# A gated attention and a low-rank mixer on one core: scores computed for the upper triangle only, transposes by DMA, and an order made by a list scheduler

## The chip, the cores and the metric

The kernel runs on one core of a Trainium2 chip. The metric is the device time of one execution in microseconds (us). Engines: TensorE (PE, with its weight loads as PEld), VectorE (DVE), ScalarE (ACT), GpSimd (POOL) and SyncE (SP, which here only issues DMAs). The one slow execution seen here (of e5) took 2.3% longer than that kernel's median. The batches ran on different chips; the kernel before took 1374.2 to 1375.3 us (medians) in all of them.

## The reference

Eight sequences of S = 3136 rows, width D = 256; z has 64 columns.

```python
scores = (1.0 / S) * z @ z.T              # symmetric, 3136 x 3136 for each sequence
attn   = maximum(scores, 0) ** 2          # symmetric too
x      = u * (attn @ v)
h      = (x.T @ U @ V).T                  # U: S x 32, V: 32 x S
uu     = x + h
out    = uu + maximum(uu @ w1, 0) @ w2    # w1: 256 x 1024, w2: 1024 x 256
```

Rows are handled in 25 tiles of 128 (the last has 64 rows). `attn` is symmetric: block (i, j) is the transpose of block (j, i). The change builds on this.

## The kernel before

All 25 x 25 blocks of the scores are computed, in groups of 512 columns, each as a matmul of 128 rows of contraction of which the upper 64 are zero. The mixer of a sequence follows its attention, and x is transposed by matmuls with an identity.

```python
for gi, (g0, gw) in enumerate(igroups):                       # groups of 512 columns
    for jp in range(0, NT, 2):
        for jj in range(npair):
            nc.tensor.matmul(out=ps_s[:, jj, :gw],
                             lhsT=zzT[:, (jp + jj) * P : (jp + jj + 1) * P],
                             rhs=zzT[:, g0 : g0 + gw], start=True, stop=True)
        # relu: every fourth on DVE, the others on ACT; then the square on DVE
        nc.scalar.activation(out=attn_sb[...], in_=ps_s[...], func=AF.Relu)
        nc.vector.tensor_tensor(out=attn_sb[...], in0=attn_sb[...], in1=attn_sb[...], op=ALU.mult)
    for qq in range(nq):                                      # attention times v
        for jt in range(NT):
            nc.tensor.matmul(out=ps_o[:, qq, :], lhsT=attn_sb[:, jt, q * P : (q + 1) * P],
                             rhs=v_bf[:, jt, :], start=(jt == 0), stop=(jt == NT - 1))
    # ... x_bf = ps_o * u; after all groups: t1 = U^T x
# mixer: x transposed by matmul and V^T t1 added in PSUM; then w1, relu on ACT, w2, add, store
nc.tensor.matmul(out=ps_u2[:, db, ...], lhsT=x_bf[:, it, db * P : (db + 1) * P], rhs=ident, ...)
# ...
emit_prep(0)
for b in range(B):
    emit_attention(b)
    if b + 1 < B:
        emit_prep(b + 1)
    emit_mixer(b)
```

## Time and profile before

| | before |
|---|---|
| time, median of 3 | 1374.39 us |
| TensorE busy | 96% of the span, at the full granted clock |
| ACT, DVE busy | 58%, 52% |
| DMA queue | 20.7% of 16 engines |
| one sequence | 168 us |

The page of the kernel before: engines with busy time, the busy tenths of 40 slices of the span, the DMA queue, and the chain of work that ended last by engine and line.

```profile
PE 1317.1 (96%) x9865; PEld 913.3 (67%) x10008; DVE 707.9 (52%) x1104; ACT 792.9 (58%) x976; POOL 23.7 (2%) x41
PE   3999999999999999999999999999999999999998
PEclk9999999999999999999999999999999999999999
DMA  9611421124111241111411115111121111111101
...
q1 hardware_dynamic: 109440, 86.41, 20.7%
...
PE 75%; ACT 21%; DMA 2%; issue 1%; DVE 1%; ACTq 0%; SPq 0%; POOL 0%
ACT relu_sb L277 12%; ACT attn_sb L184 4%; ACT u2T_bf L260 3%; ACT zzT L135 2%; DMA v_raw<-in_v_dram 1%; PE ps_6060 L202 0%; PE ps_4297 L202 0%; PE ps_11349 L202 0%; PE ps_7477 L202 0%; PE ps_2188 L202 0%; PE ps_12766 L202 0%; PE ps_11003 L
```

TensorE is busy for 90% or more of every slice but the first and the last, and the clock digit is 9 (full) throughout. The chain of the next view, in order of time (start, duration, what), gives the durations of matmuls in a steady stream:

```profile
207.46 3.07 PE ps_2015 L202 x28
...
330.31 0.86 PE ps_3405 L270 x4
```

28 matmuls of 256 columns take 3.07 us, 0.109 us from start to start; four of 512 columns 0.86 us, 0.216 us from start to start. The copy of t1, made once per sequence, shows the rhythm (count, durations in ns, first and last start):

```profile
L231 ACT CAST t_sb<-ps_3083 x1: 373/373/373, 305.6 to 305.6; 128x256 bf16<-128x256 f32 x1
L231 ACT CAST t_sb<-ps_4846 x1: 372/372/372, 473.5 to 473.5; 128x256 bf16<-128x256 f32 x1
```

473.5 - 305.6 = 167.9 us per sequence. At the two durations above, a sequence's 371,200 matmul columns need about 158 us, so bubbles are few and only less TensorE work can help much.

### The profile page before, as it was taken

The numbers are of one execution on the slowest core, as the hardware profiler recorded it, in microseconds if no ns is written. First come the engines' busy times: TensorE is split into PE (matmuls) and PEld (weight loads), VectorE is DVE, ScalarE is ACT, GpSimd is POOL, SyncE is SP. The second block draws the span as 40 slices with busy tenths as digits, with TensorE's granted clock in tenths as the row PEclk, the third lists the DMA queues.
The fourth block names the chain that finished last, engine by engine and source line by source line (L and its number), as shares of the span: only waits on it lengthen the run. The fifth ranks groups of instructions, "written<-read, shape, count | busy, mean of one in ns | idle before, by whom it ended". The sixth has DMA issues, their size and how long they took to land.

```text
span 1373.0 us, 22895 instructions
## 1 busy us (share of the span) xinstructions
PE 1317.1 (96%) x9865; PEld 913.3 (67%) x10008; DVE 707.9 (52%) x1104; ACT 792.9 (58%) x976; POOL 23.7 (2%) x41
## 2 busy tenths in 40 slices
PE   3999999999999999999999999999999999999998
PEld 1677666676666766667666676666766667666665
DVE  1776147751477414774157732677217772177721
ACT  6854855557555575556655565655655555455554
POOL 2000000000000000000000000000000000000000
PEclk9999999999999999999999999999999999999999
DMA  9611421124111241111411115111121111111101
GB/s 238 181 32 30 146 71 32 32 64 134 49 32 32 65 146 43 31 32 57 148 49 32 32 49 157 41 32 32 57 102 33 32 32 34 62 34 32 32 32 65
DMA packets 109542, 87.89 MB, mean 64 GB/s; under 512 B 32832, under 2 KB 109120, under 8 KB 109440
## 3 DMA queue, kind: packets, MB, share of 16 engines
q1 hardware_dynamic: 109440, 86.41, 20.7%
q8 instruction: 78, 1.28, 0.4%
q14 instruction: 24, 0.20, 0.0%
HBM read 60.70 MB, written 25.69 MB: 63 GB/s over the span
## 4 chain that ended last, share of the span: by engine, by line
PE 75%; ACT 21%; DMA 2%; issue 1%; DVE 1%; ACTq 0%; SPq 0%; POOL 0%
ACT relu_sb L277 12%; ACT attn_sb L184 4%; ACT u2T_bf L260 3%; ACT zzT L135 2%; DMA v_raw<-in_v_dram 1%; PE ps_6060 L202 0%; PE ps_4297 L202 0%; PE ps_11349 L202 0%; PE ps_7477 L202 0%; PE ps_2188 L202 0%; PE ps_12766 L202 0%; PE ps_11003 L202 0%; PE ps_9240 L202 0%; PE ps_5714 L202 0%; PE ps_2534 L202 0%
## 5 line engine op out<-in xcount | busy, mean ns | idle before, releaser
L202 PEld LDWEIGHTS <-attn_sb 128*128 128x128 bf16 x5000 | 466.9, 98 | 164.3 <-DVE attn_sb L189 61.9
L189 DVE TENSOR_TENSOR attn_sb<-attn_sb 128x1024 bf16<-128x1024 bf16 (+3 forms) x728 | 407.0, 608 | 73.7 <-ACT attn_sb L184 71.4
L169 PEld LDWEIGHTS <-zzT 128*128 128x128 bf16 x1400 | 133.3, 98 | 107.2 <-issue 29.3
L297 PEld LDWEIGHTS <-relu_sb 128*128 128x128 bf16 x1600 | 148.6, 98 | 50.5 <-ACT relu_sb L277 24.0
L270 PEld LDWEIGHTS <-w_bf 128*128 128x128 bf16 x896 | 83.2, 98 | 87.2 <-issue 7.8
L150 ACT CAST v_bf<-v_raw 128x1024 bf16<-128x1024 f32 (+1 forms) x56 | 52.0, 965 | 24.0 <-DMA v_raw<-in_v_dram 15.5
L246 PEld LDWEIGHTS <-x_bf 128*128 128x128 bf16 x400 | 30.3, 97 | 10.7 <-issue 4.5
L128 PEld LDWEIGHTS <-z_bf 128*128 128x128 bf16 x200 | 16.1, 102 | 26.3 <-issue 22.5
L289 PEld LDWEIGHTS <-V_bf 128*128 128x128 bf16 x200 | 19.3, 98 | 6.4
L223 PEld LDWEIGHTS <-U_bf 128*128 128x128 bf16 x200 | 19.6, 98 | 2.2
L212 POOL MEMSET u_sb<- 128x256 f32 x8 | 2.5, 311 | 1047.3 <-DVE x_bf L214 1047.3
L128 PE MATMUL ps_124<-ident,z_bf 128*128 128x128 bf16 x4 | 0.6, 299 | 19.7 <-ACT z_bf L121 19.7
L120 POOL MEMSET z_bf<- 128x1600 bf16 x8 | 11.4, 1431 | 80.8 <-PE ps_6732 L253 13.6
L121 ACT ACTIVATE z_bf<-z_raw 128x1600 bf16<-128x1600 f32 x8 | 12.4, 1550 | 0.0
L253 PEld LDWEIGHTS <-t_sb 128*128 128x128 bf16 x112 | 10.9, 97 | 1.4 <-issue 1.1
L305 DVE TENSOR_TENSOR out_sb<-ps_1522,x_bf 128x512 f32<-128x512 f32 x1 | 0.7, 692 | 16.8 <-PE ps_1522 L297 16.8
L305 DVE TENSOR_TENSOR out_sb<-ps_6811,x_bf 128x512 f32<-128x512 f32 x1 | 0.7, 692 | 16.7 <-PE ps_6811 L297 16.7
L305 DVE TENSOR_TENSOR out_sb<-ps_8574,x_bf 128x512 f32<-128x512 f32 x1 | 0.7, 692 | 16.7 <-PE ps_8574 L297 16.7
L305 DVE TENSOR_TENSOR out_sb<-ps_5048,x_bf 128x512 f32<-128x512 f32 x1 | 0.7, 690 | 16.7 <-PE ps_5048 L297 16.7
L305 DVE TENSOR_TENSOR out_sb<-ps_10337,x_bf 128x512 f32<-128x512 f32 x1 | 0.7, 692 | 16.7 <-PE ps_10337 L297 16.7
L305 DVE TENSOR_TENSOR out_sb<-ps_3285,x_bf 128x512 f32<-128x512 f32 x1 | 0.7, 690 | 16.7 <-PE ps_3285 L297 16.7
L305 DVE TENSOR_TENSOR out_sb<-ps_12100,x_bf 128x512 f32<-128x512 f32 x1 | 0.7, 690 | 16.7 <-PE ps_12100 L297 16.7
(2728 smaller groups left out, 2817.8 us busy)
## 6 DMA issues: line engine op xcount, KB each, us to landing
v_raw<-in_v_dram SPq DMA_DIRECT2D x48, 512.0 KB, 4.8
u_sb<-in_u_dram SPq DMA_DIRECT2D x96, 256.0 KB, 2.6
out_dram<-out_sb SPq DMA_DIRECT2D x96, 256.0 KB, 2.1
z_raw<-in_z_dram SPq DMA_DIRECT2D x8, 768.0 KB, 5.3
wtmp<-in_moe_w_ch_dram SPq DMA_DIRECT2D x4, 512.0 KB, 3.8
v_raw<-in_v_dram SPq DMA_DIRECT2D x8, 64.0 KB, 2.2
u_sb<-in_u_dram SPq DMA_DIRECT2D x8, 64.0 KB, 2.1
out_dram<-out_sb SPq DMA_DIRECT2D x8, 64.0 KB, 2.0
```

The costliest lines, as they stand in the source:

```text
L135: nc.scalar.copy(out=zzT[:, tg * P : (tg + n_in_g) * P], in_=pz[:, : n_in_g * P],)
L150: nc.scalar.copy(out=v_bf[:, c0 : c0 + cn, :], in_=v_raw[:, :cn, :])
L169: nc.tensor.matmul(out=ps_s[:, jj, :gw], lhsT=zzT[:, (jp + jj) * P : (jp + jj + 1) * P], rhs=zzT[:, g0 : g0 + gw], start=True, stop=True,)
L184: nc.scalar.activation(out=attn_sb[:, jp : jp + npair, :gw], in_=ps_s[:, :npair, :gw], func=AF.Relu,)
L189: nc.vector.tensor_tensor(out=attn_sb[:, jp : jp + npair, :gw], in0=attn_sb[:, jp : jp + npair, :gw], in1=attn_sb[:, jp : jp + npair, :gw] ...
L202: nc.tensor.matmul(out=ps_o[:, qq, :], lhsT=attn_sb[:, jt, q * P : (q + 1) * P], rhs=v_bf[:, jt, :], start=(jt == 0), stop=(jt == NT - 1),)
L223: nc.tensor.matmul(out=pt1[:, 0, :], lhsT=U_bf[:, it, :], rhs=x_bf[:, it, :], start=(it == 0), stop=(it == NT - 1),)
L246: nc.tensor.matmul(out=ps_u2[:, db, q * P : (q + 1) * P], lhsT=x_bf[:, it, db * P : (db + 1) * P], rhs=ident, start=(q == 0), stop=False,)
L260: nc.scalar.copy(out=u2T_bf[:, :, c0 : c0 + cw], in_=ps_u2[:, :, :cw])
L270: nc.tensor.matmul(out=ps_m1[:, hh, :cw], lhsT=w1_bf[:, db, ht * P : (ht + 1) * P], rhs=u2T_bf[:, db, c0 : c0 + cw], start=(db == 0), stop ...
L277: nc.scalar.activation(out=relu1_sb[:, hp : hp + 2, :cw], in_=ps_m1[:, :, :cw], func=AF.Relu,)
L297: nc.tensor.matmul(out=ps_f[:, qq, :], lhsT=relu1_sb[:, ht, q * P : (q + 1) * P], rhs=w2_bf[:, ht, :], start=False, stop=(ht == NH - 1),)
```

## The change

The kernel is rewritten. Its intent:

1. Scores only for the upper triangle and for the tail row of blocks. z lies twice in SBUF, in partitions 0 to 63 and 64 to 127, so that two matmuls of 64 rows of contraction run side by side in the two halves of the array.
2. The lower triangle comes from DMA transposes, SBUF to SBUF, of the squared blocks; so do z^T and the mixer's input. TensorE does no transposes.
3. Each step is a task. A list scheduler, run when the program is built, simulates the engines with fitted durations and fixes every engine's order; the mixer of one sequence fills TensorE's gaps in the next attention.
4. Squared scores live in 64 slots of 512 columns. All loads but a few of the first sequence, and all stores, are issued on POOL.

The diff has over 1100 lines; these are its core (cuts marked).

```diff
+NSLOT = 64
+def t_mm(n):
+    return n / 2400.0 + 0.0025
 ...
+            s = sq[c, k] = add(f"sq{b}.{c}.{k}", {"DVE": t_dve(cols)}, ..., deps=[it.relu], ...)
 ...
+                    ts = tslot[c, k]
+                    tr[c, k] = add(
+                        f"tr{b}.{c}.{k}", {"SP": 0.25 + 0.12 * blocks},
+                        lambda K, t, ...: K.tr_quad(t, q, ts, k, cols),
+                        deps=[s], prio=0.5, pipe=0.18 * blocks, use=[q, ts],
+                    )
 ...
+    def score(self, t, row, col0, cols, zT):
+        z = self.zT[zT.i]
+        a = slice(64 * t.half, 64 * t.half + 64)
+        self.nc.tensor.matmul(
+            out=self.pair[t.pref.i][:, t.half, :cols],
+            lhsT=z[a, row * P : (row + 1) * P], rhs=z[a, col0 : col0 + cols], start=True, stop=True,
+        )
 ...
+    def tr_quad(self, t, q, ts, k, cols):
+        a = P if k == 0 else 0
+        self.nc.sync.dma_start_transpose(
+            out=self.q[ts.i][:, a:cols].rearrange("p (t r) -> p t r", r=P), in_=self.q[q.i][:, a:cols]
+        )
 ...
+    plan = make_plan()
+    with tc.manual_schedule():
+        bufs = Bufs(tc.nc, ctx, tc, u, v, z, moe_U, moe_V, moe_w_ch1, moe_w_ch2, out)
+        for t in plan.order:
+            t.emit(bufs, t)
```

## The prediction

> **What bounds it now.** TensorE. The page gives matmul busy 96% of 1373.0 us at granted clock 1.00; ACT 58%, DVE 52%, DMA queue 1 20.7%. The timeline shows a steady rhythm: the t1 copy recurs every 168 us, one sequence. Counting columns of the matmuls: 371,200 per sequence (scores 80,000, attention times v 160,000, mixer products 102,400, the rest transposes by matmul, t1 and V products). The chain of waits has 28 matmuls of 256 columns in 3.07 us (0.109 us each) and four of 512 in 0.86 us (0.216 us). At these rates the work is about 158 us, so only some 10 us per sequence are bubbles, plus about 27 us of start. Less TensorE work is the only large lever.
>
> **What the change does to TensorE, per sequence (estimates from those two durations).**
> - Scores: only the upper triangle and the tail row, 41,600 columns in place of 80,000, and with 64-deep contraction on row halves two run at once. The Trainium skill, "TensorEngine Tiling (Array Packing)", section Tiling Modes / Key Properties, allows two 64-row tiles in parallel and says that changing the mode drains the array; no run here shows it yet. About 46 pairs: 10 us, plus 3 to 4 us for some 17 mode changes (0.2 us each, my guess). Before: 34 us.
> - z and x transposes go to DMA: 4 us off. The added V product in the transposed layout and its repetition in the output group fall into one 25-matmul product: about 3 us off. t1 on four column groups: 1.5 us in place of 2.7.
> - Attention times v stays: 625 x 0.109 = 68 us. Mixer products stay: 43.4 us.
> Sum: about 129 us in place of 158. Eight times: 1033 us.
>
> **What moves elsewhere.** DMA gains, per sequence, 363 transposed 128x128 bf16 blocks (25 z, 276 scores, 24 half ones for the tail, 50 u), 11.9 MB. At the 261 GB/s of the skill's "DMA: Bandwidth & Descriptors", section Latency and other measured facts, that is 46 us (an estimate; no run shows it); the plain 10.8 MB at the page's rate (86.41 MB in 20.7% of the span, 304 GB/s) is 36 us. Together 82 us of about 130: not a bound unless transposes cost twice that. ACT and DVE: score relus fall from 643 us to about 390, squares from 407 to about 225, the PSUM copies (28 + 48 us) vanish, x+h adds and casts bring about 90 us; some 1130 us on two engines, about 52% each. Not a bound.
>
> **Critical path.** All TensorE savings lie on it. The mixer of one sequence is laid into the next attention, so relu waits there (ACT relu_sb is 12% of the chain) should be covered. Start shrinks to about 12 us (weights load later). The last mixer runs alone: about 12 us of fill and drain. Static order, transposes landing late and single-slot buffers will cost stalls: 4% of 1033, about 40 us.
>
> **Predicted: 1095 us, range 1055 to 1165. Faster by over 2%: 0.96; within: 0.02; slower: 0.02.**
>
> **Right if:** TensorE stays over 90% busy with about 129 us of work per sequence; 1400 score matmuls become 728, overlapped in pairs; attention times v still 5000 at 0.109 us; DMA busy near 65%, transposes landing in 2 to 4 us. **Wrong if:** idle before attention times v is put down to transposes (DMA over 85% or landing over 6 us, SP issue the limit); score pairs do not overlap; DVE over 75% busy; loads from POOL late[...]; the last mixer costs over 70 us.

## The result, and the profile after

The changed kernel took 1263.22 us (median of 4 runs, 1258.97 to 1267.25; before, 1374.4 us). The ratio of the fast runs is 0.9194, 95% interval 0.917 to 0.9217: 8% faster, where 20% was predicted. A ratio is the mean time of one kernel's fast runs over that of the other's in the same rounds, so it is not quite the ratio of the medians. Executions over 1.5% slower than the fastest of the same kernel are left out of the means.

The page of the changed kernel, the same lines, the two big DMA queues (q1: issued by SP, q0: by POOL), and the group of transposes among the DMA issues (count, median us from issue to landing):

```profile
PE 1084.5 (86%) x8533; PEld 770.1 (61%) x8624; DVE 611.3 (48%) x1400; ACT 513.0 (41%) x817; POOL 177.9 (14%) x247
PE   1646793899988999889987999868989899899998
PEclk9968897999988999999988999989999999999999
DMA  8487864976669957797569867798568885577232
...
q1 hardware_dynamic: 401648, 97.70, 46.7%
q0 software_dynamic: 24496, 83.97, 25.1%
...
PE 57%; DMA 21%; issue 14%; DVE 2%; SPq 2%; POOL 2%; ACT 2%; POOLq 0%; ACTq 0%; DVEq 0%
...
q<-q SPq DMA_TRANSPOSE x664, 3.2
```

TensorE is no longer always busy (86%; the prediction asked for over 90%), its clock digits drop to 6 to 8 in places, DMA takes 21% of the chain where it took 2%, and the DMA engines are 46.7 + 25.1 = 72% busy. A table by stretch of time (start:end, length, busy time of each engine, granted clock, DMA share, GB/s) shows where:

```profile
0.00:45.00 45.00, 8.41 (x31) 2.26 (x32) 14.28 (x42) 16.47 (x28) 4.62 (x10) 1.00 0.72 151
90.00:135.00 45.00, 32.01 (x204) 19.91 (x204) 15.03 (x38) 12.05 (x23) 6.30 (x8) 0.77 0.86 163
320.00:466.00 146.00, 135.05 (x1075) 97.73 (x1086) 75.70 (x173) 62.56 (x101) 21.21 (x29) 0.95 0.78 154
1170.00:1263.00 93.00, 84.30 (x673) 62.07 (x680) 28.54 (x45) 34.02 (x37) 14.14 (x20) 0.99 0.25 77
```

The first attention, with no mixer to fill the gaps, does badly: 32.01 us of 45 busy, at a clock of 0.77, the lowest of these stretches. A sequence in the middle takes 146 us with TensorE busy for 135 of them; 168 us before. The last stretch holds the end of the last attention (its last matmul ends at 1202.4 us) and the last mixer; TensorE is busy for 91% of it.

Three lines of the list of waits (engine, its line, what it waited for; us in total, times, longest) name what TensorE waited for:

```profile
PE acc L748 <- DMA q<-q: 67.0, 48, 7.3
PE pair L816 <- DMA uT<-ubf: 41.9, 9, 14.1
PE pair L716 <- DMA zT<-zbf: 27.4, 1, 27.4
```

All three are transposes: of scores, of the mixer's input, and the first one of z. Adding up every gap of TensorE in the trace gives 173.1 us of idle time (52.6 before).

From the trace I split each span into three: TensorE idle; time lost to a lowered clock (its busy time multiplied with the share of the clock not granted just then); and the rest, work at full clock.

```
                 span     idle   clock   work at full clock   (us)
before         1373.0     52.6     1.6   1318.8
after          1263.3    173.1    39.0   1051.2
predicted      1095    62 together       1033
```

(The 3 to 6 us after the last matmul are counted as work here.) The work is what was predicted, within 2%. The idle time and the clock are not. The Trainium skill, "TensorE: Matmul & The Clock Gate", Part 1, says that an idle window drops the array to half its clock; this trace agrees that the loss is one half: its records of the granted clock are 1.0 or 0.5, never between. It also shows that the array had not always stood still before: in the 3.4 us before each of the 20 stretches at half clock TensorE was busy for 0 to 1.8 us. So idle time cost more than its own length here: 39 us on top of 173 us.

### What the transposes' issue looks like

An issue is the time that SP spends on handing one transpose to the DMA engines; it lands when its data have arrived. The trace's records of the score transposes on the SP queue (durations in ns: minimum, median, maximum), and of the mixer's, of eight blocks each:

```profile
L735 SPq DMA_TRANSPOSE q<-q x664: 1119/1208/5080, 32.3 to 1174.4; - x166
DMA to landing us min/median/max: 2.2/3.2/17.8
...
L806 SPq DMA_TRANSPOSE uT<-ubf x48: 1232/1254/2503, 217.4 to 1241.5; - x48
```

Sorted by the number of 128x128 blocks (worked out from the trace's records matched with the scheduler's tasks; the 56 of the tail rows, 1188 and 1199 ns in the median, are left out):

```
blocks in one transpose    count    median issue ns
1                             48    1184
2 (scores)                    48    1197
3                            208    1199
4                            360    1216
8 (mixer)                     48    1254
12 (z, first half)             8    2450
13 (z, second half)            8    1503
```

Up to eight blocks, an issue costs nearly the same whatever it moves. z's 16 cost more, the first of each sequence 2450 ns; why is not shown. The scheduler believed 0.25 + 0.12 per block: 0.37 us for one block, 0.73 us for four. From the start of one transpose to the start of the next the median is 1.31 us. The 784 issues take 1041.9 us in all, and in stretches of 25 us from 50 to 1175 us the SP queue spent 80 to 95% of the time in them (69% in one), not counting the short gap that follows each.

### The profile page after: what moved, and what is told of

It reads as the page before. It is cut to its first block, busy times and chain, and to the rows that moved or that the text cites. A ratio compares the mean times of both kernels' runs of the same rounds, so it can differ in the third digit from the quotient of the medians.

```text
span 1263.3 us, 22331 instructions
## 1 busy us (share of the span) xinstructions
PE 1084.5 (86%) x8533; PEld 770.1 (61%) x8624; DVE 611.3 (48%) x1400; ACT 513.0 (41%) x817; POOL 177.9 (14%) x247
## 3 DMA queue, kind: packets, MB, share of 16 engines
q1 hardware_dynamic: 401648, 97.70, 46.7%
q0 software_dynamic: 24496, 83.97, 25.1%
## 4 chain that ended last, share of the span: by engine, by line
PE 57%; DMA 21%; issue 14%; DVE 2%; SPq 2%; POOL 2%; ACT 2%; POOLq 0%; ACTq 0%; DVEq 0%
PE acc L748 31%; DMA q<-q 13%; PE acc L838 10%; PE pair L816 8%; PE pair L716 5%; DMA zT<-zbf 4%; DMA stg<-in_z_dram 2%; PE pair L777 1%; SPq L735 1%; DMA uT<-ubf 1%; DVE q L731 1%; POOL out_dram L855 1%; ACT zbf L635 1%; DMA stg<-in_v_dram 1%; ACT r L827 1%
## 5 line engine op out<-in xcount | busy, mean ns | idle before, releaser
L748 PE MATMUL acc<-v,q 128*128 128x256 bf16 x4808 | 621.3, 279 | 74.4 <-DMA q<-q 67.0
L748 PEld LDWEIGHTS <-q 128*128 128x128 bf16 x4808 | 466.0, 100 | 232.4 <-DMA q<-q 86.9
L725 ACT ACTIVATE q<-pair 128x512 bf16<-128x512 f32 (+3 forms) x533 | 261.6, 554 | 346.2 <-PE pair L716 328.9
L827 ACT ACTIVATE r<-pair 128x1024 bf16<-128x1024 f32 (+1 forms) x200 | 198.2, 1005 | 295.5 <-PE pair L816 291.8
L731 DVE TENSOR_TENSOR q<-q 128x512 bf16<-128x512 bf16 (+3 forms) x728 | 246.3, 388 | 37.7 <-ACT q L725 36.4
L816 PE MATMUL pair<-uT,w1b 128*128 128x512 bf16 (+1 forms) x805 | 201.1, 361 | 48.9 <-DMA uT<-ubf 41.9
L727 DVE TENSOR_SCALAR q<-pair 128x512 bf16<-128x512 f32 (+2 forms) x195 | 121.3, 634 | 216.8 <-PE pair L716 192.3
L838 PE MATMUL acc<-w2b,r 128*128 128x256 bf16 x1600 | 195.7, 276 | 0.1
L838 PEld LDWEIGHTS <-r 128*128 128x128 bf16 x1600 | 157.9, 99 | 25.6 <-issue 2.8
L716 PE MATMUL pair<-zT 64*128 64x512 bf16 (+3 forms) x728 | 113.2, 371 | 42.3 <-DMA zT<-zbf 27.4
```

The source lines that it names most:

```text
L716: self.nc.tensor.matmul(out=self.pair[t.pref.i][:, t.half, :cols], lhsT=z[a, row * P : (row + 1) * P], rhs=z[a, col0 : col0 + cols], start ...
L725: self.nc.scalar.activation(out=o, in_=i, func=AF.Relu)
L727: self.nc.vector.tensor_single_scalar(out=o, in_=i, scalar=0.0, op=ALU.max)
L731: self.nc.vector.tensor_tensor(out=o, in0=o, in1=o, op=ALU.mult)
L748: self.nc.tensor.matmul(out=self.acc[acc.i][:, :D], lhsT=src[:, w : w + P], rhs=self.v[v.i][:, j, :], start=first and n == 0, stop=last an ...
L816: self.nc.tensor.matmul(out=o, lhsT=self.w1b[:, e, ht * P : (ht + 1) * P], rhs=r, start=e == 0, stop=e == ND - 1)
```

## The experiments

Twelve kernels were run. All are edits of the changed kernel. Theory A holds the issue on SP for the limit, B the DMA engines and the loads, C the order that came of wrong constants; D and B2 were formed on the way.

### e1_split: the same bytes in more transposes

```diff
-        self.nc.sync.dma_start_transpose(
-            out=self.q[ts.i][:, a:cols].rearrange("p (t r) -> p t r", r=P), in_=self.q[q.i][:, a:cols]
-        )
+        m = a + (cols - a) // P // 2 * P
+        for lo, hi in ((a, m), (m, cols)):
+            if hi > lo:
+                self.nc.sync.dma_start_transpose(
+                    out=self.q[ts.i][:, lo:hi].rearrange("p (t r) -> p t r", r=P), in_=self.q[q.i][:, lo:hi]
+                )
```

> Theory A (the SP queue is the limit: each transpose takes about 1.2 us to issue and 1.30 us from start to start, whatever its size): the same bytes in 1400 issues instead of 784, so 1400 x 1.30 = 1820 us and with head and tail 1850 to 2000 us. Theory B (the DMA engines or the loads beside the transposes are the limit): bytes unchanged, 1240 to 1330 us. Theory C (the order is wrong because the scheduler's constants are): order unchanged, 1240 to 1330 us.

Measured: 1975.42 us, correct, one run. The page's engines, its clock, and the queue of SP:

```profile
PE 1284.5 (65%) x8624; PEld 790.5 (40%) x8624; DVE 615.1 (31%) x1400; ACT 516.3 (26%) x817; POOL 178.1 (9%) x247
...
PEclk9657785778867797688967789688995879778899
...
q1 hardware_dynamic: 421360, 97.78, 26.3%
```

The megabytes are those of before the edit (97.78 against 97.70), the engines are less busy with them (26.3% of a longer span), and the time rose by 712 us for 616 more issues, 1.16 us each. B and C are refuted for this step: issues, not bytes, were added, and issues cost. The clock fell to 0.797 in the mean: 200.7 us were lost to it in place of 39.0, which is 162 of the 200 us by which TensorE's busy time rose for the same work.

### e2_merge: the same bytes in fewer transposes

Two neighbouring 512-column slots are allocated together and one transpose covers both: 472 issues in place of 784.

```diff
-        self.q = many("q", NSLOT, [P, 512], BF16)
+        self.qq = many("q", NSLOT // 2, [P, 1024], BF16)
+        self.q = [t[:, h : h + 512] for t in self.qq for h in (0, 512)]
 ...
+def place(refs, free):       # slots 2i and 2i+1 lie side by side: a pair takes both
 ...
+            elif (k % 2 or k == last_k) and (c, k0) in tslot:
+                wide = (k - k0) * 512 + cols
+                tr[c, k] = tr[c, k0] = add(f"tr{b}.{c}.{k}", {"SP": 1.3}, ...,
+                    deps=[sq[c, k0], s] if k > k0 else [s], ...)
```

> One transpose over two neighbouring 512-column slots: 472 issues instead of 784, the same bytes, the same 64 slots. A: 472 x 1.30 = 614 us of issue, no longer the limit; pairs of slots are harder to find and cost some stalls, so 1150 to 1215 us. B: 1240 or more, since no byte less moves and each landing takes longer. C does not speak against a gain here, as the scheduler's constants are then near the measured ones.

Measured: 1283.38 us (1276.79 to 1286.12), ratio 0.9328, interval 0.9296 to 0.936. That is 1.6% slower than the change itself; each of its four fast runs is above each of the change's: the expectation of theory A failed, and B's "1240 or more" came true. Yet the issue did shrink:

```profile
L769 SPq DMA_TRANSPOSE q<-q x376: 1120/1240/7675, 35.1 to 1197.4; - x188
DMA to landing us min/median/max: 2.3/3.3/16.8
...
PE 1098.1 (86%) x8624; PEld 773.1 (60%) x8624; DVE 594.6 (46%) x1358; ACT 534.5 (42%) x859; POOL 178.9 (14%) x247
```

An issue of up to eight blocks has a median of 1240 ns, so the SP queue issued for 720.6 us in all, and from 75 to 1100 us it was between 33 and 96% busy in stretches of 25 us. TensorE idled as much as before the edit (177.7 us). Taken alone this run speaks for B. The reading kept here is that the SP queue was full in the changed kernel, as e1 says, but not alone: another limit lay right behind. e5 tests it. The kernel's scheduler, which here has the right cost for an issue, by itself gives this order 1170 us, and 1095 us to the change's. A pair of slots is held until the last of its blocks is used, and the scores come in 202 bursts (runs of score matmuls) in place of 171.

### e3_noloads: no loads of u and v after the first sequence

```diff
     def load_v(self, t, b, k, st):
+        if b:
+            return
 ...
     def load_u(self, t, b, k, u):
+        if b:
+            return
```

> u and v are loaded for the first sequence only (a wrong result on purpose), the 784 transposes stay. A: gains only what the loads add to the issue itself (issues summed to 1042 us against 784 x 1.20 = 941 us), so 1150 to 1230 us with the SP queue still over 90% busy. B: the waits of TensorE for transposes vanish and the time comes to about 1100 us with the SP queue idle a good part.

Measured: 1224.86 us, one run, a wrong result. The issues still took 1021.9 us and TensorE idled 138.2 us. So the loads account for 38 us here; with 784 issues in the way, taking them off entirely gives no more. This fits A and refutes B as the first limit.

### e4_cost11: the scheduler told of the cost

```diff
-                        f"tr{b}.{c}.{k}", {"SP": 0.25 + 0.12 * blocks},
+                        f"tr{b}.{c}.{k}", {"SP": 1.1},
```

(The other three transposes' costs are changed in the same way, to 1.1 and, for z, 1.6. At 1.2 and 1.3 the scheduler finds no order: both accumulators are taken by attention that waits for the mixer's buffers.)

> The scheduler is told that an issue costs 1.1 us whatever its size (at 1.2 and 1.3 it ends in a deadlock), so the order changes and nothing else. A: the number of issues is the same, 1235 to 1290 us. C: the right constant gives a better order, 1200 us or less.

Measured: 1276.36 us, correct, one run. C is refuted as far as 1.1 us can tell, also if this run was a slow one (2.3% less would be 1248 us): knowing the cost does not help while the issues are as many.

### e5_merge70: more slots for the merged transposes

```diff
-NSLOT = 64
+NSLOT = 70
-        ("q", NSLOT), ..., ("stg", 3), ..., ("ob", 3), ...
+        ("q", NSLOT), ..., ("stg", 2), ..., ("ob", 2), ...
```

Six slots of 1 KB per partition, paid for with one staging buffer of 4 KB and one output buffer of 2 KB.

> e2 freed the SP queue and gained nothing. Theory D: what took its place is the slots, since a transpose over two slots holds four at once; the scheduler of e2 already foresaw it by its own count of bursts (202 in place of 171). With 70 slots in place of 64 (paid for with one staging and one output buffer less, bursts back to 166) D expects 1190 to 1225 us. Theory B2: what took its place is the landing of transposes beside the loads; then more slots help little, 1255 to 1285 us.

Measured: 1190.37 us (median of 5; the slowest, 1217.43), ratio of the fast runs 0.8677, interval 0.8646 to 0.8707. That is the low end of D's range: 93 us less than e2, 73 us less than the change. Slots were the second limit. No run gave the change its six slots with all 784 issues, so what slots alone bring is not measured; the scheduler, by its own account, sees no gain in that (1098.6 us against 1094.8, with the same two buffers given up).

### e6_merge70_noloads: the same without the loads

The edit of e3 on e5.

> e5 without the loads of u and v after the first sequence (a wrong result on purpose). If loads beside transposes are what remains (B2), the time falls by 60 us or more against e5, to 1150 or less. If not, it falls by 20 to 40 us, as e3 did against the changed kernel.

Measured: 1103.24 us, one run, a wrong result: 87 us less than e5. In the changed kernel the same edit took off 38 us. Once the issues and the slots are out of the way, the loads are what is left. The page:

```profile
PE 1040.7 (94%) x8543; PEld 761.6 (69%) x8624; DVE 607.0 (55%) x1399; ACT 517.9 (47%) x818; POOL 106.8 (10%) x149
...
PEclk9999999999999999999999999999999999999999
```

TensorE idles 54.6 us and loses 3.3 us to the clock. The transposes now start when the scheduler means them to. Start of the same transposes in the scheduler's plan and in the trace:

```
                              plan    trace    late (us)
change, tr4.0.1 (784 issues)  491.7    607.7   116.0
change, tr7.7.0               935.7   1109.9   174.2
e6, tr4.15.2 (472 issues)     601.1    604.5     3.4
e6, tr7.12.1                  976.6    979.6     3.0
```

Without the loads the plan holds (no transpose is more than 11.2 us late). What it had wrong is the cost of an issue, and what a load does to the transposes beside it. The trace of the change shows the second directly: 64 of its 664 score transposes took over 6 us to land, and every one of them had packets of POOL's queue beside it, as 65% of all had.

### e7_act_loads and e8_sp_loads: the same loads in smaller packets

In the trace of the change, the DMA packets of the two queues (median ns of one; 95th percentile):

```
                                 bytes   median ns   95%
transposes (SP)                    256       18       31
loads and stores from POOL        4096      165      664
loads from SP (first sequence)    1024       51       78
```

The Trainium skill, "DMA: Bandwidth & Descriptors", section Queues, rings and completion order, says that each DMA engine takes turns between its queues packet by packet, where a packet is a run of several descriptors (single pieces of a transfer). If the trace's records are such packets, which is not known, a transpose beside a POOL load gets one of 18 ns for each of 165 ns. Loads of v and u issued on ACT or SP come in packets of 1024 bytes, those of z in packets of 256. e7 issues the loads of z, v and u on ACT, e8 on SP:

```diff
-                f"vld{b}.{k}", {"POOL": 1.1} if b or k % 2 else {"SP": 0.45},
+                f"vld{b}.{k}", {"ACT": 0.15},          # e8: {"SP": 0.45}
-                    f"uld{b}.{c // 4}", {"POOL": 1.1}, ...
+                    f"uld{b}.{c // 4}", {"ACT": 0.15}, ...
```

> e5 with the loads of z, v and u issued on the ACT queue in place of POOL (stores stay). In the trace a POOL load moves in packets of 4096 bytes, 159 to 165 ns each, a transpose in packets of 256 bytes, 18 ns each; loads on a hardware queue move in packets of 1024 bytes, 44 to 46 ns. Theory B2a (the DMA engines take turns packet by packet, so a transpose beside a POOL load gets 18 ns in every 180): with smaller load packets transposes land sooner, 1125 to 1170 us. Theory B2b (the bytes of the loads take their time whatever the packets): 1180 to 1200 us.

> e5 with the loads of z, v and u on the SP queue, in one line with the transposes. B2a: no more turns between loads and transposes, but a transpose stands behind a whole load and SP may wait for a buffer: 1130 to 1190 us. B2b: 1180 to 1210 us.

Measured: e7 1130.52 us, e8 1127.65 us, one run each, both correct. (The scheduler makes its order anew for each, of much the same length by its own account: 1100 and 1099 us, e5 1101.) That is some 60 us less than e5 for the same bytes. The queues of e7 (q10 is ACT's; packets, MB, share of 16 engines):

```profile
q1 hardware_dynamic: 386816, 95.22, 51.6%
q10 hardware_dynamic: 77440, 57.81, 19.1%
q0 software_dynamic: 8832, 28.60, 7.5%
```

57.81 MB in 77440 packets are 747 bytes a packet; q0 in the change had 83.97 MB in 24496, 3428 bytes. TensorE's idle time is 71.1 us in e7 and 69.3 us in e8, the loss to the clock 14.2 and 12.6 us. B2b, the bytes as such, would have left e5's time, so moving the loads off POOL's queue is what helped. Turns by packet would explain e7, but that is argued, not shown. e8, where loads and transposes stand in one queue, is as fast. Another thing changed with the queue: the issue of a u load took 766 ns on POOL (median, in the change), 375 ns on ACT (e7) and 533 ns on SP (e8). Which part of the gain is the packets and which the issue, these runs do not separate.

### e9_act_only: small load packets, and all 784 issues

The edit of e7 on the changed kernel itself.

> The changed kernel with its 784 transposes and 64 slots, only the loads of z, v and u issued on ACT. If the issue of transposes is still the first limit, the small load packets give no more than taking the loads away gave (e3, 1225 us): 1215 to 1260 us. If the loads were the first limit all along, about 1130 us as in e7.

Measured: 1238.27 us, correct, one run. The same edit that gave about 60 us after e5 gives 25 us here. A slow state of 2.3% could hide some 28 us more, which still is far from 1130. The order of the limits matters: the issues came first. These two kernels have the same transposes, so their traces show what the loads' queue does to them: the median landing of a score transpose stays (3.2 us in the change, 3.1 here), the longest falls from 17.8 to 8.4 us.

### e10_sp_all: the stores on SP too

```diff
-                    f"st{b}.{k}.{h}", {"POOL": 1.1},
+                    f"st{b}.{k}.{h}", {"SP": 0.45},
```

> e8 with the stores on the SP queue too, so that nothing is left in 4096-byte packets. If packets are what counts, a further 5 to 15 us: 1110 to 1125 us; if SP then waits for store buffers before it issues transposes, slower than e8's 1127.7 us.

Measured: 1122.7 us, correct, one run: 5 us less than e8, at the small end of what was expected. Single runs of one kernel differ by as much, so the stores' part stays unproved.

### e11_v_after_z: the first v loads behind z's first transpose

```diff
-                deps=[after(b - 1, 6 + 2 * k)] if b else [],
+                deps=[after(b - 1, 6 + 2 * k)] if b else ztr[:1],
```

> e8 with the first v loads behind the first transpose of z, which landed after 13.0 us in the changed kernel beside them. It should land after about 4 us, TensorE start some 5 to 8 us earlier than at 26 us, and the time fall by 0 to 8 us: 1118 to 1130 us.

Measured: 1137.8 us, 10 us slower than e8. TensorE did start earlier, but only at 19.3 us in place of e8's 21.0 (moving the loads had already shortened that wait from 27.4 us), and its idle time over the whole span was larger, 77.5 us against 69.3. The first transpose of z landed after 5.4 us (6.9 in e8), not 4. The expectation failed, and the edit is dropped; 10 us between two single runs of unknown state are not enough to call it slower.

### e12_final: the best version in five rounds

> The kernel of e10 again, timed in five rounds: 1115 to 1130 us in the fast state, a ratio of 0.81 to 0.825 to the kernel before.

Measured: 1122.75 us (1119.17 to 1126.04), ratio to the kernel before 0.8158, interval 0.8146 to 0.8169; correct. It beats both kernels. Its page, and its score transposes:

```profile
PE 1051.5 (94%) x8542; PEld 766.5 (68%) x8624; DVE 601.3 (53%) x1385; ACT 522.7 (46%) x832; POOL 7.8 (1%) x14
PE   1878999999899998999999999999999999999998
...
PEclk9998999999999999999999999999999999999999
...
PE 78%; DMA 4%; issue 1%; SPq 1%; DVE 1%; ACT 0%; DVEq 0%; ACTq 0%
...
DMA to landing us min/median/max: 2.2/3.2/7.3
```

TensorE is 94% busy. The median landing is that of the change (3.2 us), but the longest is 7.3 us where it was 17.8, and TensorE waited 12.9 us for score transposes where it had waited 67.0. DMA fell from 21% of the chain to 4%.

The whole account, from the traces (SP issue is the sum of all transposes' issue times):

```
             time us   issues   SP issue    idle   clock    work
after        1263.22     784     1041.9    173.1    39.0   1051.2
e2_merge     1283.38     472      720.6    177.7    39.3   1064.5
e3_noloads   1224.86     784     1021.9    138.2    29.8   1055.2
e9_act_only  1238.27     784     1023.5    152.5    36.1   1047.8
e6           1103.24     472      638.3     54.6     3.3   1043.6
e7           1130.52     472      654.7     71.1    14.2   1043.4
e12_final    1122.75     472      659.1     68.9    14.0   1041.4
```

(idle, clock and work are of the profiled execution, whose span differs a little from the median.)

## Why the prediction was right or wrong

- **What bounded the kernel before**: right. Less TensorE work was what could help, and the change is faster.
- **TensorE's work after**: right. Predicted 1033 us, measured 1051.2 us of work at full clock (1041.4 in e12). The score pairs do overlap: the two matmuls of a pair start 3 to 4 ns apart and pairs of 512 columns follow each other every 0.226 us at full clock, close to one matmul alone before (0.216 us). The skill's "TensorEngine Tiling (Array Packing)", section Tiling Modes / Key Properties, said that such tiles run in parallel; this trace agrees. t1's 25 matmuls on four column groups start within 0.67 us, where 1.5 us stood in the prediction.
- **ACT and DVE**: right. Predicted 1130 us on the two, measured 513.0 + 611.3 = 1124.3 us.
- **DMA load**: named as no bound "unless transposes cost twice that", and mis-sized. The transposes' queue was busy 46.7% of 1263.3 us, 74 us per sequence, where 46 us stood in the prediction; with q0 the engines are 72% busy, not 65%. That alone did not set the time: e12 moves the same bytes in 1123 us.
- **Stalls: the step that failed**, "Static order, transposes landing late and single-slot buffers will cost stalls: 4% of 1033, about 40 us". With start and end, idle time and clock were predicted at 62 us; they were 173.1 + 39.0 = 212.1 us. The difference of 150 us, with 18 us more work, is the whole error of 168 us. The 4% was a guess, and the sum that could have replaced it was never made: the prediction counted the transposes in blocks and bytes and not in instructions. Per sequence there are 98 of them, and 98 x 1.31 us is 128 us on one in-order queue, as much as TensorE's 129 us, with no slack left for waits on slots and squares. "SP issue the limit" does stand among the signs of being wrong, without a number.
- **Behind it stood two more**: slots for the squared scores, as soon as transposes hold pairs (e2 against e5, 93 us), and the loads on POOL's queue beside the transposes (e5 against e7 and e8, about 60 us; that their large packets are the reason is argued, not shown). The loads' share depends on the others: 25 us while the issue is full (e9).
- **The clock** was not thought of: stalls lowered it to 0.951 in the mean, 39 us.
- **Start of about 12 us**: wrong, TensorE's first matmul came at 27.4 us. The first transpose of z took 13.04 us to land beside the first loads, as the start of the chain shows (start, duration, what):

```profile
0.74 3.67 DMA stg<-in_z_dram
6.03 13.04 DMA zT<-zbf
21.08 6.30 DMA zT<-zbf
27.43 1.05 PE pair L716 x4
```

- **The last mixer**: right; from the last attention matmul, at 1202.4 us, to the end TensorE is busy for 52.1 of 60.9 us, so 8.8 us are idle where 12 were predicted.
- **Loads from POOL late**: not seen in their issue; POOL's issues of the 512 KB u loads took 766 ns in the median and 773 at the ninetieth percentile.

What stays open: how a DMA engine divides its time among queues was inferred from packets and times, not seen packet by packet; whether six more slots would have helped with 784 issues; and e12's remaining 83 us of idle and clock, of which 26.2 us of idle time fall in the first 50 us.

## What to carry to other kernels

Count DMA instructions as well as bytes, and multiply by the measured start-to-start time on their queue: a queue in strict order is an engine like the others, and it can be full while every page of engine shares looks idle. Removing the first limit can gain nothing until the second goes too, so when more of a thing hurts (e1) and less of it does not help (e2), look for what stands right behind before dropping the theory. Where bulk loads run beside small transfers that an engine waits for, try another queue for the loads: here ACT's or SP's in place of POOL's took off 60 us.

## What the Trainium skill lacked or had wrong

- "DMA: Bandwidth & Descriptors" gives sequencer times for a transpose only in its part on another chip's faster path, beside those of "previous generations", and there as one command per tile for SBUF to SBUF. No page has the issue time as measured on this chip: 1.18 us for one 128x128 block, 1.25 us for eight, but 1.50 us for z's thirteen and 2.45 us for its twelve, and 1.31 us from start to start.
- The same page's section Latency and other measured facts has 261 GB/s for DMA transposes. Here the transposes' queue moved 97.70 MB in 46.7% of 1263.3 us, 166 GB/s while busy (174 in e6, with most loads gone). "Advanced Engine Details and Errata", X-Bar Transpose, calls transposes as fast as regular DMAs; POOL's loads and stores moved 83.97 MB in 25.1%, 265 GB/s. The size of the packets may be the whole difference: in the kernel before, z's plain loads in packets of 256 bytes took 18 ns a packet in the median, as the transposes do here.
- The same page's rules say that spreading DMAs over SP, ACT and GpSimd does not help bandwidth. Which queue issues a load does matter to the transposes: moving the loads from POOL to ACT or SP took off about 60 us of 1190 (e5 against e7 and e8). POOL's packets have 4096 bytes, those of v and u on ACT and SP 1024; the packet-wise turns that the page describes would fit that, but no run shows them.
